# Attention and soft experts on one core: another order of the attention's steps and loads, and one cast split between ScalarE and GpSimd

## The chip, the cores and the metric

The kernel runs on one core of a Trainium2 chip. The metric is the time of one execution on the device in microseconds (us); lower is better. The engines go by their short names: PE is TensorE's matmul, PEld its weight load, DVE is VectorE, ACT is ScalarE, POOL is GpSimd, SP is SyncE, which issues the transfers (DMAs).

## The reference

Attention over q, k, v of shape (4, 8, 768, 64): 4 batches, 8 heads, 768 positions. Each query sees the first 8 keys and the 96 keys up to its own position; a bias proportional to the distance, with a slope of its own for each head, is added. Then a mixture of 8 experts with 4 slots each, in which every slot is a softmax-weighted sum over all 3072 tokens:

```python
scores = scale * (q @ k.T) + bias            # masked outside the window
a = exp(scores - max); a /= a.sum(-1) + 1e-9
x = (a @ v) as 3072 x 512                    # heads side by side
logits = x @ phi                             # 512 x 32 slots
slot_input = softmax(logits, axis=0).T @ x   # over all tokens
slot_out = relu(slot_input @ w1[e]) @ w2[e]  # w1: 512 x 1024, w2: 1024 x 512
out = softmax(logits, axis=1) @ slot_out
```

The weights are 32 MB in float32, the queries, keys and values some 20 MB as laid out, the output 6 MB.

## The kernel before

**Units.** The 32 heads are taken in 16 pairs (units u = 0 to 15, four to a batch; i = 0, 1 is the head of the pair). A unit's work is cut into named steps, each a few instructions of one engine:

- `load_qk`, `load_v` (lines 424, 427): transfers of queries with keys (832 KB) and of values (448 KB) into one of two buffers each; units 2 and 3 have buffers of their own.
- `scores(u, k)`, k = 0, 1, 2 (L571, PE): 8, 8 or 12 float32 matmuls into one of two PSUM banks `sc`, in turn. `biased(u, k)` (L580, DVE): adds the bias table and keeps the running maximum, from the bank to `tb`, and so frees the bank.
- `max_t` (L587, PE), `max_r` (L592, DVE): the maximum over all, from `biased(u, 2)`. `exponential(u, i)` (L596, ACT): in place in `tb`.
- `w_hi(u, i)` (L599, ACT): the weights as float16, high part, into `ph`, for all three parts of 432 columns at once. `w_lo(u, i, part)` (L606): what the rounding left over, on POOL, or as `w_lo_dve` on DVE, for one part.
- `v_hi` (L539, POOL), `v_hi_act` (L542, ACT) or `v_hi_dve` (DVE), and `v_lo` (L549, DVE): the same split of the values.
- `values(u, i)` (L623, PE): 39 float16 matmuls, high by high, high by low, low by high. There is one buffer `ph` for each i, so `w_hi(u+1, i)` waits for `values(u, i)`; v_hi and v_lo have two, so unit u waits for values of u-2.
- `ev_sums`, `ev_recs` (or `ev_sum`, `ev_rec` for one head) and `ev_mul` (L639, L645, L651, DVE): divide by the sums, into `xn`. `tr(u, k)` (L663, PE): transposes; `tr_copy(u, k)` (L668, ACT) or `tr_copy_dve` (L672, DVE): out of PSUM, 480 columns for k = 0 and 288 for k = 1. `logits` (L693, PE) and, once a batch, the running softmax over tokens: `logits_all`, `strip_max`, `strip_exp`, `by_token`, `dispatch`.
- `warm` (L560, PE): matmuls on constants, at the start.

**What sets the order.** `ORDER` (line 55) is one list of all these steps. The program walks it and issues each step's instructions on its engine, so each engine's queue holds its steps in the list's order, and an instruction that waits holds all behind it on that engine. SP's queue holds the transfers in the list's order too: `load_qk`, `load_v`, and the pieces of the experts' weights: `piece(k)` (1 MB into one of ten free tiles), `extra(i)` (the unused ends of tiles still in use) and `free(i)` (a tile, or a part of one, of which the attention has made its last use). All run through `load_w` (line 413).

**After the list.** `last_dispatch` finishes the last batch, then comes the experts' part: `hidden_part` (L104: 128 matmuls of 512 columns), `project` (L159), the combination with the token weights (L205), copies out (L218) and the output's transfers (L221). In it, tiles whose w1 part is used up take the last eight w2 pieces, in two halves each: 17 transfers on `wp`, the second halves last, which only the last projection reads.

Of the kernel before, what the change touches and what calls it, by code (L numbers as in the profile page):

```python
# [28 lines left out]
QW = KB + WIN  # L29
# [278 lines left out]
def tile_attention_moe(ctx: ExitStack, tc: tile.TileContext, qk, v, phi, w1, w2, nn, out):  # L308
    nc = tc.nc
# [58 lines left out]
    phi_ = [t[:, 0:PH].bitcast(F16) for t in pht]  # L368
# [11 lines left out]
    held = []  # L380
    for name, i, *_ in ORDER:
        if name == "free":
# [70 lines left out]
    def blocks(w):  # L453
        return w[:, 0:6 * PB].rearrange("p (s c) -> p s c", c=PB)
# [19 lines left out]
    def late_constants():  # L474
        nc.gpsimd.tensor_tensor(out=i4, in0=ident[:, 0:32], in1=ident[:, 32:64], op=ALU.add)
        nc.gpsimd.tensor_tensor(out=i4, in0=i4, in1=ident[:, 64:96], op=ALU.add)
        nc.gpsimd.tensor_tensor(out=i4, in0=i4, in1=ident[:, 96:128], op=ALU.add)
        nc.gpsimd.tensor_copy(out=by_row.rearrange("p (s j) -> p s j", s=4), in_=ident.rearrange("p (s r) -> p s r", s=4)[:, :, 0:NS // 4])
        nc.gpsimd.memset(sl, 0.0)
        moe.constants()  # L480
# [18 lines left out]
    def tb(u):  # L499
        return tbuf[u % 3]  # L500
# [53 lines left out]
    def warm_x(u):  # L554
        for n in (256, 256, P):
            nc.tensor.matmul(out=xx[:, 0, 0:n], lhsT=idb[:, 0:P], rhs=idb[:, 0:n], start=True, stop=True)
# [31 lines left out]

    def max_r(u):
        m = ms.pop((u, "m"))[:, 0:P]  # L590
        nbs[u] = nb = wk.tile([P, 1], F32, name="nb", tag="nb", bufs=2)
        nc.vector.tensor_tensor_reduce(out=m, in0=m, in1=shift.to_broadcast([P, P]), scale=-T_SC, scalar=3.0e38, op0=ALU.add, op1=ALU.min, accum_out=nb)  # L592

    def exponential(u, i):
        t = tb(u)[:, i]
        nc.scalar.activation(out=t, in_=t, func=AF.Exp, bias=nbs[u], scale=T_SC)  # L596

    def w_hi(u, i):
        nc.scalar.copy(out=blocks(phi_[i])[:, :, 0:QW], in_=tb(u)[:, i].rearrange("p (s c) -> p s c", c=QW))  # L599

    def w_hi_dve(u, i):
        nc.vector.tensor_copy(out=blocks(phi_[i])[:, :, 0:QW], in_=tb(u)[:, i].rearrange("p (s c) -> p s c", c=QW))

    def w_lo(u, i, part, engine=None):
        c = slice(2 * part, 2 * part + 2)
        (engine or nc.gpsimd).tensor_tensor(out=blocks(plo_[i])[:, c, 0:QW], in0=tb(u)[:, i].rearrange("p (s c) -> p s c", c=QW)[:, c],  # L606
                                            in1=blocks(phi_[i])[:, c, 0:QW], op=ALU.subtract)

    def w_lo_dve(u, i, part):
        w_lo(u, i, part, nc.vector)  # L610

    def values(u, i):
        ph, pl = phi_[i], plo_[i]
        vh, vl = vhi[u % 2], vlo[u % 2]
        x = sums(u, i)
        ops = []
        for t in range(NJ):
            for j, c in ((t, PCOL[t]), (t - 1, PCOL[t - 1] + KB)):
                if j >= 0:
                    for w, vv, d in ((ph, vh, D + 1), (ph, vl, D), (pl, vh, D + 1)):  # L620
                        ops.append((t, c, w, vv, j, d))
        for z, (t, c, w, vv, j, d) in enumerate(ops):
            nc.tensor.matmul(out=x[:, (D + 1) * t:(D + 1) * t + d], lhsT=w[:, c:c + P], rhs=vv[:, j, i, 0:d],  # L623
                             start=(z == 0), stop=(z == len(ops) - 1), skip_group_check=True)
# [253 lines left out]

    def table_rest_act(u):
        table.rest(nc.scalar.copy)  # L880

    def table_pair_act(p):
        table.pair_act(p)

    def table_pair(p):
        table.pair(p)

    steps = dict(piece=piece_of, free=free, extra=extra, load_phis=load_phis, bcast=bcast, keys=keys, table_rest=table_rest, table_rest_act=table_rest_act, table_pair_act=table_pair_act, warm_x=warm_x, warm=warm,
                 table_even=table_even, table_odd=table_odd, table_pair=table_pair, load_qk=load_qk, load_v=load_v, v_hi=v_hi, v_hi_act=v_hi_act, v_hi_dve=v_hi_dve, v_lo=v_lo,
                 scores=scores, biased=biased, max_t=max_t, max_r=max_r, exponential=exponential, w_hi=w_hi, w_lo=w_lo, w_lo_dve=w_lo_dve, w_hi_dve=w_hi_dve,  # L890
                 values=values, ev_sum=ev_sum, ev_rec=ev_rec, ev_sums=ev_sums, ev_recs=ev_recs, ev_mul=ev_mul, tr=tr, tr_copy=tr_copy, tr_copy_dve=tr_copy_dve,
                 logits=logits, logits2=logits2, logits_half=logits_half, logits_all=logits_all, strip_max=strip_max, strip_exp=strip_exp,
                 strip_sum=strip_sum, by_token=by_token, by_token_copy=by_token_copy, lnat_copy=lnat_copy, dispatch=dispatch, dispatch_sum=dispatch_sum)
    late_constants()
    for name, u, *args in ORDER:
        steps[name](u, *args)
    left = LeftBanks()
    put_rest = last_dispatch(left, lambda: warm_x(last))
    att.close()


    tail = ExitStack()
# [327 lines left out]
```

## Time and profile before

| | |
|---|---|
| median of 3 runs | 185.04 us (184.34 to 185.16) |
| profiled execution | 184.54 us, span 182.5 us |
| PE busy (x2805) | 170.5 us, 93% |
| PEld busy | 125.8 us, 69% |
| DVE busy (x378) | 141.6 us, 78% |
| ACT busy (x164) | 125.8 us, 69% |
| POOL busy (x129) | 97.2 us, 53% |
| moved by DMA | 61.41 MB, mean 337 GB/s |

The span is from the first to the last instruction of the profiled execution. A busy share is the engine's time in instructions; matmuls are pipelined, so PE's is not a measure of how full the array is. The granted clock of PE is full (2.4 GHz) as long as PE works. In the timeline a row is one step or a run of equal instructions, with its start, its length and, in brackets, the idle time before it and what ended it.

### The profile page before, as it was taken

To read this page: it belongs to the slowest core of one execution; us is meant where nothing else is said; L and a number is where in the kernel's file an instruction comes from. 1 tells how busy PE (TensorE), PEld (TensorE's weight loads), DVE (VectorE), ACT (ScalarE), POOL (GpSimd) and SP (SyncE) were. 2 spreads that over 40 slices of the span, in tenths; PEclk is the share of its full clock that TensorE was granted. 3 is DMA by queue.
4 is the path that set the end of the run, shared out by engine and by line. 5 is a ranking of instruction groups with operands and counts; after the bars stand their busy time and mean duration, and the time that the engine had idled before them with its cause. 6 is when DMAs were issued, how large, how long until landed. Compare 5 with 4: busy or idle time off the path is not lost.

```text
span 182.5 us, 6745 instructions
## 1 busy us (share of the span) xinstructions
PE 170.5 (93%) x2805; PEld 125.8 (69%) x2805; DVE 141.6 (78%) x378; ACT 125.8 (69%) x164; POOL 97.2 (53%) x129
## 2 busy tenths in 40 slices
PE   8999899999999999999999998999899999999820
PEld 2567689797878877979888986875533256677710
DVE  5999999999998989899999999987867303346430
ACT  3499989999989999988999999953302120345320
POOL 6926689859799498797998996750010000000000
PEclk9999999999999999999999999999999999999975
DMA  6999999958998956789887399999999999989892
GB/s 186 420 399 390 413 400 392 392 192 307 381 391 338 383 156 247 250 310 379 288 344 276 89 310 376 407 370 416 416 387 409 408 404 404 380 303 405 347 334 65
DMA packets 15306, 61.41 MB, mean 337 GB/s; under 512 B 1698, under 2 KB 2850, under 8 KB 13474
## 3 DMA queue, kind: packets, MB, share of 16 engines
q1 hardware_dynamic: 15264, 60.89, 87.8%
q8 instruction: 24, 0.39, 0.9%
q14 instruction: 16, 0.13, 0.2%
q10 hardware_dynamic: 2, 0.00, 0.0%
HBM read 54.59 MB, written 6.29 MB: 334 GB/s over the span
## 4 chain that ended last, share of the span: by engine, by line


## 5 line engine op out<-in xcount | busy, mean ns | idle before, releaser
L606 POOL TENSOR_TENSOR ph<-tb,ph 128x432 f16<-128x432 f32 x83 | 85.9, 1066 | 18.9 <-ACT ph L599 15.8
L596 ACT ACTIVATE tb<-tb,nb 128x1296 f32<-128x1296 f32 x32 | 43.7, 1374 | 0.9 <-DVE nb L592 0.8
L623 PEld LDWEIGHTS <-ph 128*128 128x128 f16 x1248 | 40.7, 97 | 4.2 <-issue 2.8
L599 ACT CAST ph<-tb 128x1296 f16<-128x1296 f32 x32 | 40.6, 1271 | 2.8 <-PE x L623 0.9
L623 PE MATMUL x<-v,ph 128*128 128x65 f16 (+1 forms) x1209 | 42.0, 193 | 0.3 <-POOL ph L606 0.2
L571 PE MATMUL sc<-raw 64*128 64x216 f32 (+1 forms) x392 | 40.8, 340 | 0.0
L571 PEld LDWEIGHTS sc<-raw 64*128 64x128 f32 x392 | 32.3, 186 | 6.0 <-issue 3.5
L651 DVE CUSTOM_DVE_ANT_1 xn<-x,rc 120x448 f32<-120x448 f32 x31 | 18.3, 622 | 2.1 <-PE m L774 1.6
L580 DVE CUSTOM_DVE_ANT_1 tb<-sc,tt,mx 128x864 f32<-128x864 f32 x16 | 17.8, 1115 | 1.1 <-DVE mx L580 0.5
L549 DVE SCALAR_TENSOR_TENSOR v<-vt,v 128x896 f16<-128x896 f32 x14 | 16.2, 1159 | 0.0
L663 PE MATMUL m<-ident,xn 120*128 120x120 f32 x98 | 14.7, 276 | 0.2 <-DVE xmax L651 0.2
L663 PEld LDWEIGHTS m<-ident,xn 120*128 120x128 f32 x98 | 10.0, 141 | 2.7 <-issue 1.5
L104 PE MATMUL hp<-wp,sl 128*32 128x512 f32 x80 | 10.9, 594 | 0.3 <-ACT sl L99 0.3
L606 DVE TENSOR_TENSOR ph<-tb,ph 128x432 f16<-128x432 f32 x13 | 9.6, 765 | 0.0
L580 DVE CUSTOM_DVE_ANT_1 tb<-sc,xtt,mx 128x864 f32<-128x864 f32 x8 | 8.9, 1115 | 0.4 <-DVE mx L580 0.2
L580 DVE CUSTOM_DVE_ANT_1 tb<-sc,xta,mx 128x864 f32<-128x864 f32 x8 | 8.9, 1112 | 0.2
L542 ACT ACTIVATE v<-vt 128x896 f16<-128x896 f32 x9 | 8.6, 951 | 0.0
L205 PE MATMUL cp<-sos,ct 32*128 32x128 f32 (+1 forms) x120 | 8.4, 334 | 0.2 <-ACT ph L218 0.2
L159 PE MATMUL o<-wp,ht 128*32 128x128 f32 x256 | 8.4, 275 | 0.0
L580 DVE CUSTOM_DVE_ANT_1 tb<-sc,tt 128x864 f32<-128x864 f32 x8 | 8.4, 1050 | 0.0
L159 PEld LDWEIGHTS o<-wp,ht 128*32 128x32 f32 x256 | 6.6, 109 | 1.5 <-issue 1.0
L910 POOL MEMSET ht<- 128x536 f32 x1 | 0.5, 544 | 13.1 <-PE ld L848 13.1
(235 smaller groups left out, 283.5 us busy)
## 6 DMA issues: line engine op xcount, KB each, us to landing
raw<-in_qk_dram SPq DMA_DIRECT2D x14, 832.0 KB, 5.7
wp<-in_w_dram SPq DMA_DIRECT2D x10, 1024.0 KB, 8.0
wp<-in_w_dram SPq DMA_DIRECT2D x15, 512.0 KB, 9.0
vt<-in_v_dram SPq DMA_DIRECT2D x14, 448.0 KB, 5.5
tb<-in_w_dram SPq DMA_DIRECT2D x3, 1024.0 KB, 8.1
wp<-in_qk_dram SPq DMA_DIRECT2D x2, 832.0 KB, 9.5
raw<-in_w_dram SPq DMA_DIRECT2D x2, 832.0 KB, 4.5
ph<-in_w_dram SPq DMA_DIRECT2D x2, 768.0 KB, 9.9
```

The lines of the kernel that those rows point to most:

```text
L104: self.nc.tensor.matmul(out=hp[n][32 * s:32 * s + 32, :], lhsT=slv(a, c, s), rhs=w1(4 * a + s, c // 2)[:, (c % 2) * DF + 512 * n:(c % 2) * ...
L159: nc.tensor.matmul(out=o[32 * s:32 * s + 32, o0:o0 + w], lhsT=ht[:, k:k + 32], rhs=w2(4 * a + s, half)[:, at:at + w], start=(a == 0 and c ...
L542: nc.scalar.activation(out=vhi[u % 2][:, :, :, 0:D], in_=vraws(u), func=AF.Copy, scale=V_SC)
L549: nc.vector.scalar_tensor_tensor(out=vlo[k].rearrange("p j i d -> p (j i) d"), in0=vraws(u).rearrange("p j i d -> p (j i) d"), scalar=V_SC ...
L571: nc.tensor.matmul(out=z[:, i, at:at + n], lhsT=r_[r, KCOL[j]:KCOL[j] + KR], rhs=r_[r, KW + KB * j:KW + KB * j + n], start=True, stop=True)
L580: nc.vector.tensor_tensor_reduce(out=tb(u)[:, :, BW * k:BW * k + BW], in0=sc[(3 * u + k) % 2][:, :, 0:BW], in1=table.unit(u % NP, k), scal ...
L596: nc.scalar.activation(out=t, in_=t, func=AF.Exp, bias=nbs[u], scale=T_SC)
L599: nc.scalar.copy(out=blocks(phi_[i])[:, :, 0:QW], in_=tb(u)[:, i].rearrange("p (s c) -> p s c", c=QW))
L606: (engine or nc.gpsimd).tensor_tensor(out=blocks(plo_[i])[:, c, 0:QW], in0=tb(u)[:, i].rearrange("p (s c) -> p s c", c=QW)[:, c], in1=bloc ...
L623: nc.tensor.matmul(out=x[:, (D + 1) * t:(D + 1) * t + d], lhsT=w[:, c:c + P], rhs=vv[:, j, i, 0:d], start=(z == 0), stop=(z == len(ops) - ...
L651: nc.vector.tensor_tensor_reduce(out=xnb[(u // 2) % 3][:, :, c:c + D], in0=by_query(u, i)[:, :, 0:D], in1=rcs.pop((u, i)).unsqueeze(2).to_ ...
L663: nc.tensor.transpose(out=m[:, at:at + KB], in_=xnb[(u // 2) % 3][:, t, P * (p % 2):P * (p % 2) + P], identity=ident[0:KB, 0:KB])
```

## The change

The list gets another order, on all engines. Some steps change engine: `v_hi` of units 8 and 9 goes from ScalarE to GpSimd, that of unit 10 from GpSimd to ScalarE and that of unit 15 from GpSimd to VectorE; of the 32 `tr_copy`, VectorE has 7 in place of 8, one of them with 480 columns in place of three; 13 of the 96 `w_lo` stay on VectorE, but others. `w_hi(15, 0)` is split: part 0 on ScalarE, parts 1 and 2 on GpSimd. The order in which SP issues pieces and loads from unit 6 on was

piece 4, piece 1, qk 6, piece 6, qk 7, piece 3, v 6, qk 8, piece 0, v 7, qk 9, piece 2, v 8, qk 10, piece 7, v 9, qk 11, v 10, qk 12, piece 5, v 11, qk 13, piece 9, v 12, qk 14, piece 8, v 13, qk 15, v 14, v 15

and becomes

qk 6, piece 4, qk 7, piece 1, v 6, piece 6, qk 8, v 7, qk 9, v 8, qk 10, piece 3, v 9, piece 0, qk 11, v 10, qk 12, piece 2, v 11, piece 7, qk 13, piece 5, v 12, piece 9, qk 14, v 13, piece 8, qk 15, v 14, v 15.

The order of the 18 `free` was 0, 14, 11, 1, 9, 3, 16, 4, 10, 7, 17, 6, 2, 8, 13, 5, 12, 15 and becomes 0, 14, 11, 9, 1, 3, 16, 4, 7, 10, 17, 2, 8, 15, 5, 12, 6, 13; which piece lies in which tile follows from it. `warm`, the number of matmuls, and all that comes after the list stay.

The list is one line in the code; here it is broken, and cut to its beginning, the steps around units 2 and 3, those around unit 10, and the last pairs:

```diff
 ORDER = [
-    ('load_qk', 0), ('load_v', 0), ('load_qk', 1), ('load_v', 1), ('load_v', 3), ('load_qk', 2),
-    ('extra', 8), ('bcast', 0), ('load_qk', 3), ('keys', 0), ('load_v', 2), ('extra', 1),
+    ('load_qk', 0), ('bcast', 0), ('load_v', 0), ('load_qk', 1), ('load_v', 1), ('load_v', 3),
+    ('load_qk', 2), ('extra', 8), ('load_qk', 3), ('keys', 0), ('table_even', 0), ('load_v', 2),
+    ('extra', 1), ('warm', 0, 6),
...
-    ('w_lo', 0, 0, 0), ('w_hi', 0, 1), ('max_r', 1), ('w_lo_dve', 0, 0, 2), ('scores', 2, 2), ('exponential', 1, 0), ('biased', 2, 1),
-    ('w_lo', 0, 1, 0), ('values', 0, 0), ('w_lo_dve', 0, 1, 1), ('scores', 3, 0), ('w_hi', 1, 0), ('w_lo_dve', 0, 1, 2), ('v_lo', 1),
-    ('values', 0, 1), ('exponential', 1, 1), ('w_lo', 1, 0, 0), ('biased', 2, 2), ('load_v', 5), ('extra', 4), ('w_lo', 1, 0, 1),
-    ('w_hi', 1, 1), ('piece', 4), ('ev_sums', 0), ('ev_recs', 0), ('max_t', 2), ('biased', 3, 0), ('scores', 3, 1),
-    ('extra', 3), ('w_lo', 1, 0, 2), ('extra', 7), ('v_hi_act', 2), ('ev_mul', 0, 0), ('extra', 2), ('scores', 3, 2),
+    ('w_lo', 0, 0, 0), ('scores', 2, 2), ('biased', 2, 2), ('v_lo', 1), ('w_lo', 0, 1, 0), ('w_lo', 0, 1, 2), ('values', 0, 0),
+    ('w_hi', 1, 0), ('load_qk', 4), ('w_lo', 1, 0, 0), ('exponential', 1, 1), ('w_lo', 1, 0, 1), ('w_lo', 1, 0, 2), ('values', 0, 1),
+    ('ev_sums', 0), ('w_hi', 1, 1), ('w_lo', 1, 1, 1), ('ev_recs', 0), ('scores', 3, 0), ('ev_mul', 0, 0), ('biased', 3, 0),
+    ('max_t', 2), ('v_hi_act', 2), ('scores', 3, 1), ('load_v', 5), ('extra', 4), ('scores', 3, 2),
...
-    ('load_v', 11), ('logits_all', 7), ('w_hi', 10, 1), ('w_lo', 10, 1, 0), ('v_lo', 10), ('values', 9, 0), ('v_hi_act', 11),
-    ('max_t', 11), ('scores', 12, 2), ('strip_max', 7), ('strip_exp', 7), ('w_lo', 10, 1, 1), ('ev_sums', 9), ('ev_recs', 9),
-    ('ev_mul', 9, 1), ('scores', 12, 1), ('ev_mul', 9, 0), ('max_r', 11), ('by_token', 7), ('w_lo', 10, 1, 2), ('w_hi', 10, 0),
-    ('values', 10, 1), ('load_qk', 13), ('by_token_copy', 7), ('biased', 12, 1), ('w_lo', 10, 0, 0), ('scores', 13, 0), ('exponential', 11, 1),
-    ('w_hi', 11, 1), ('w_lo', 10, 0, 2), ('lnat_copy', 7), ('w_lo', 11, 1, 0), ('w_lo', 11, 1, 2), ('w_lo_dve', 10, 0, 1), ('piece', 9),
-    ('load_v', 12), ('w_lo', 11, 1, 1), ('biased', 12, 2), ('v_lo', 11), ('values', 10, 0), ('ev_sums', 10), ('load_qk', 14),
-    ('exponential', 11, 0), ('w_hi', 11, 0), ('w_lo', 11, 0, 0), ('max_t', 12), ('max_r', 12), ('dispatch', 7),
...
+    ('max_t', 11), ('w_hi', 10, 1), ('v_lo', 10), ('w_lo', 9, 0, 1), ('values', 9, 0), ('scores', 12, 2), ('w_lo', 10, 1, 1),
+    ('w_lo', 10, 1, 2), ('max_r', 11), ('w_hi', 10, 0), ('exponential', 11, 1), ('ev_sums', 9), ('scores', 12, 1), ('by_token', 7),
+    ('ev_recs', 9), ('ev_mul', 9, 0), ('ev_mul', 9, 1), ('tr', 9, 1), ('by_token_copy', 7), ('v_hi_act', 11), ('w_lo_dve', 10, 1, 0),
+    ('values', 10, 1), ('lnat_copy', 7), ('w_lo', 10, 0, 1), ('piece', 7), ('w_lo', 10, 0, 0), ('biased', 12, 1), ('load_qk', 13),
+    ('scores', 13, 0), ('w_lo', 10, 0, 2), ('values', 10, 0), ('w_hi', 11, 1), ('w_lo', 11, 1, 2), ('w_lo', 11, 1, 0), ('w_lo', 11, 1, 1),
...
-    ('biased', 15, 2), ('tr', 10, 1), ('tr_copy', 10, 1), ('max_t', 15), ('ev_sums', 13), ('ev_recs', 13), ('ev_mul', 13, 0),
-    ('logits', 11), ('max_r', 15), ('ev_mul', 13, 1), ('tr', 13, 1), ('strip_sum', 3), ('logits_all', 11), ('strip_max', 11),
-    ('w_hi', 14, 0), ('tr_copy_dve', 13, 1), ('exponential', 15, 1), ('w_lo', 14, 1, 1), ('w_lo', 14, 1, 2), ('values', 14, 1), ('free', 9),
-    ('tr', 12, 1), ('strip_exp', 11), ('w_lo_dve', 14, 0, 1), ('w_lo', 14, 0, 0), ('w_hi', 15, 1), ('w_lo', 15, 1, 0), ('tr_copy', 12, 1),
-    ('by_token', 11), ('lnat_copy', 11), ('w_lo', 15, 1, 2), ('w_lo_dve', 14, 0, 2), ('values', 14, 0), ('tr', 12, 0), ('v_lo', 15),
-    ('by_token_copy', 11), ('dispatch', 11), ('free', 3), ('ev_sums', 14), ('ev_recs', 14), ('tr_copy_dve', 12, 0), ('free', 16),
-    ('ev_mul', 14, 1), ('exponential', 15, 0), ('w_hi', 15, 0), ('ev_mul', 14, 0), ('w_lo_dve', 15, 0, 1), ('w_lo_dve', 15, 0, 0), ('w_lo_dve', 15, 0, 2),
-    ('tr', 13, 0), ('free', 4), ('w_lo', 15, 1, 1), ('values', 15, 1), ('ev_sum', 15, 1), ('ev_rec', 15, 1), ('ev_mul', 15, 1),
-    ('values', 15, 0),
+    ('biased', 15, 2), ('free', 9), ('values', 13, 1), ('w_hi', 14, 1), ('strip_sum', 3), ('w_lo_dve', 14, 1, 1), ('w_lo', 13, 0, 2),
+    ('w_lo', 14, 1, 2), ('w_lo', 14, 1, 0), ('tr', 11, 1), ('tr', 11, 0), ('free', 1), ('tr_copy', 11, 1), ('tr_copy', 11, 0),
+    ('values', 13, 0), ('ev_sums', 13), ('ev_recs', 13), ('w_hi', 14, 0), ('max_t', 15), ('w_lo', 14, 0, 1), ('max_r', 15),
+    ('exponential', 15, 1), ('free', 3), ('logits', 11), ('ev_mul', 13, 0), ('ev_mul', 13, 1), ('logits_all', 11), ('strip_max', 11),
+    ('w_lo_dve', 14, 0, 0), ('tr', 12, 1), ('tr_copy', 12, 1), ('values', 14, 1), ('v_hi_dve', 15), ('v_lo', 15), ('strip_exp', 11),
+    ('w_hi', 15, 1), ('w_lo_dve', 15, 1, 0), ('w_lo_dve', 15, 1, 2), ('free', 16), ('tr', 13, 1), ('tr_copy', 13, 1), ('w_lo', 14, 0, 2),
+    ('by_token', 11), ('lnat_copy', 11), ('by_token_copy', 11), ('free', 4), ('values', 14, 0), ('free', 7), ('exponential', 15, 0),
+    ('w_hi_part_pool', 15, 0, 2), ('free', 10), ('w_hi_part', 15, 0, 0), ('w_lo_dve', 15, 1, 1), ('tr', 12, 0), ('ev_sums', 14), ('ev_recs', 14),
+    ('dispatch', 11), ('ev_mul', 14, 0), ('ev_mul', 14, 1), ('strip_sum', 7), ('free', 17), ('tr_copy', 12, 0), ('values', 15, 1),
+    ('tr', 13, 0), ('w_hi_part_pool', 15, 0, 1), ('w_lo_dve', 15, 0, 1), ('tr_copy', 13, 0), ('w_lo', 15, 0, 0), ('ev_sum', 15, 1), ('ev_rec', 15, 1),
+    ('tr', 14, 1), ('w_lo', 15, 0, 2), ('free', 2), ('ev_mul', 15, 1), ('values', 15, 0),
...
 ]
...
+    def w_hi_part(u, i, part, copy=nc.scalar.copy):
+        c = slice(2 * part, 2 * part + 2)
+        copy(out=blocks(phi_[i])[:, c, 0:QW], in_=tb(u)[:, i].rearrange("p (s c) -> p s c", c=QW)[:, c])
+
+    def w_hi_part_dve(u, i, part):
+        w_hi_part(u, i, part, nc.vector.tensor_copy)
+
+    def w_hi_part_pool(u, i, part):
+        w_hi_part(u, i, part, nc.gpsimd.tensor_copy)
...
```

## Rows read from the trace of the kernel before

**Rows 1.** Windows: stretch, length; busy us of PE, PEld, DVE, ACT, POOL; clock; DMA; GB/s

```profile
4.00:124.00 120.00, 118.37 (x2026) 96.72 (x2026) 113.27 (x291) 108.80 (x119) 94.27 (x112) 1.00 0.88 331
...
132.30:173.50 41.20, 40.57 (x674) 23.09 (x674) 18.01 (x47) 10.44 (x27) 0.54 (x1) 1.00 0.98 383
...
80.00:85.00 5.00, 5.00 (x111) 4.15 (x111) 4.92 (x15) 4.41 (x5) 3.63 (x5) 1.00 0.87 311
```

**Rows 2.** Timeline of PE, steps that nothing holds: start, us, what

```profile
6.04 1.73 PE L571 MATMUL sc<-raw 64*128 64x216 f32 x16
7.71 0.59 PE L560 MATMUL x<-const-bfloat16-1.0 128*1 128x512 bf16 x2
...
11.14 1.81 PE L571 MATMUL sc<-raw 64*128 64x216 f32 x20
12.88 1.25 PE L560 MATMUL x<-const-bfloat16-1.0 128*1 128x512 bf16 x5
...
46.68 1.00 PE L571 MATMUL sc<-raw 64*128 64x216 f32 x8
47.61 1.36 PE L623 MATMUL x<-v,ph 128*128 128x65 f16 x39
48.81 0.51 PE L663 MATMUL m<-ident,xn 120*128 120x120 f32 x3
```

**Rows 3.** Timeline of PE, steps that something holds

```profile
21.54 0.32 PE L587 MATMUL m<-ident,mx 128*128 128x128 f32 x1 [0.57 <-DVE mx L580]
21.79 2.10 PE L571 MATMUL sc<-wp 64*128 64x216 f32 x20
23.91 1.33 PE L623 MATMUL x<-v,ph 128*128 128x65 f16 x39
...
86.72 1.55 PE L623 MATMUL x<-v,ph 128*128 128x65 f16 x39
88.20 1.00 PE L571 MATMUL sc<-raw 64*128 64x216 f32 x8
```

**Rows 4.** Timeline of DVE around 20 and 103 us

```profile
18.27 1.18 DVE L606 TENSOR_TENSOR ph<-tb,ph 128x432 f16<-128x432 f32 x2
...
20.37 1.11 DVE L580 CUSTOM_DVE_ANT_1 tb<-sc,xta,mx 128x864 f32<-128x864 f32 x1
...
102.91 1.89 DVE L549 SCALAR_TENSOR_TENSOR v<-vt,v 128x896 f16<-128x896 f32 x1
```

**Rows 5.** Groups by line: what, count, busy us, mean ns, idle before

```profile
L606 POOL TENSOR_TENSOR ph<-tb,ph 128x432 f16<-128x432 f32 x83 | 85.9, 1066 | 18.9 <-ACT ph L599 15.8 <-DVE v L549 2.0 <-PE sc L571 1.1
L599 ACT CAST ph<-tb 128x1296 f16<-128x1296 f32 x32 | 40.6, 1271 | 2.8 <-PE x L623 0.9 <-POOL ph L606 0.6
L651 DVE CUSTOM_DVE_ANT_1 xn<-x,rc 120x448 f32<-120x448 f32 x31 | 18.3, 622 | 2.1 <-PE m L774 1.6
L549 DVE SCALAR_TENSOR_TENSOR v<-vt,v 128x896 f16<-128x896 f32 x14 | 16.2, 1159 | 0.0
L542 ACT ACTIVATE v<-vt 128x896 f16<-128x896 f32 x9 | 8.6, 951 | 0.0
L539 POOL TENSOR_SCALAR v<-vt 128x896 f16<-128x896 f32 x5 | 4.8, 955 | 3.4 <-PE x L623 2.8 <-DMA vt<-in_v_dram 0.6
L668 ACT COPY xtt<-m 128x480 f32<-128x480 f32 (+1 forms) x7 | 3.5, 513 | 0.8 <-PE m L663 0.8
```

**Rows 6.** Timeline of ACT and DVE at the last pair

```profile
117.97 1.40 ACT L596 ACTIVATE tb<-tb,nb 128x1296 f32<-128x1296 f32 x1
...
120.87 1.64 DVE L606 TENSOR_TENSOR ph<-tb,ph 128x432 f16<-128x432 f32 x3
```

**Rows 7.** Line 413 after 133 us (issue ns, first and last start, landing), PE's timeline

```profile
L413 SPq DMA_DIRECT2D wp<-in_w_dram x17: 327/328/1166, 135.0 to 151.6; - x17
...
DMA to landing us min/median/max: 7.3/9.0/11.0
...
167.96 2.17 PE L159 MATMUL o<-wp,ht 128*32 128x128 f32 x72
```

More of the change, by code (lines that the diff above doesn't have):

```diff
@@ L889, in tile_attention_moe @@
                  table_even=table_even, table_odd=table_odd, table_pair=table_pair, load_qk=load_qk, load_v=load_v, v_hi=v_hi, v_hi_act=v_hi_act, v_hi_dve=v_hi_dve, v_lo=v_lo,
-                 scores=scores, biased=biased, max_t=max_t, max_r=max_r, exponential=exponential, w_hi=w_hi, w_lo=w_lo, w_lo_dve=w_lo_dve, w_hi_dve=w_hi_dve,
+                 scores=scores, biased=biased, max_t=max_t, max_r=max_r, exponential=exponential, w_hi=w_hi, w_lo=w_lo, w_lo_dve=w_lo_dve, w_hi_dve=w_hi_dve, w_hi_part=w_hi_part, w_hi_part_dve=w_hi_part_dve, w_hi_part_pool=w_hi_part_pool,
                  values=values, ev_sum=ev_sum, ev_rec=ev_rec, ev_sums=ev_sums, ev_recs=ev_recs, ev_mul=ev_mul, tr=tr, tr_copy=tr_copy, tr_copy_dve=tr_copy_dve,
```

2 lines of the change are left out of this document (1 added, 1 removed).

## Prediction

> **What bounds the kernel now.** First the page: its busy shares put TensorE far ahead, but a share over the whole span hides the stages, so next the table of windows [rows 1]. From 4 to 124 us, the attention, TensorE is busy 118.37 of 120 us, VectorE 113.27, ScalarE 108.80, GpSimd 94.27: four engines near full, and the reader is to see that TensorE alone has almost no idle time. From 132.3 to 173.5 us, the experts' part, TensorE is busy 40.57 of 41.20 and nothing else is above half; no step of the change lies there. Between them are 8.3 us of small dependent steps.
>
> A busy matmul row need not mean that TensorE sets the pace, so I read its timeline step by step [rows 2]. scores(7,0) starts at 46.68 and hands over to values(4,1) at 47.61, which hands over to the next transposes at 48.81: 0.93 and 1.20 us from start to start, no gap. So in the attention the end is set by TensorE's own work plus the places where it is held. The clearest of those [rows 3]: 0.57 us of idle at 21.54, where max_t(2) waits for biased(2,2); scores(3,1) and scores(3,2), which take 2.12 us (21.79 to 23.91) where the same pair of another head pair took 1.74 (11.14 to 12.88) [rows 2]; values(10,1), 1.48 us (86.72 to 88.20) instead of 1.20. Idle time in 4 to 124 us is 1.63 us in all, 120 less 118.37; with the 0.38 and 0.28 us by which those two are drawn out, some 2.3 us is about all that a better order can win by holding TensorE less.
>
> **The change part by part.** Nothing is computed that was not computed before. What moves between engines, over the whole list [rows 5]: ScalarE loses one v_hi (0.95), two thirds of w_hi(15,0) (0.85 of 1.27) and one tr_copy of 288 columns, and gains two of 480 columns (0.51 each; the shorter one at most that): about -1.1 us. VectorE gains v_hi(15) and one short copy and loses two long ones, which about offset; v_hi on VectorE isn't in the trace. The same 896 elements took 0.95 us on ScalarE, 0.96 on GpSimd and 1.16 in VectorE's own two-input form. I take 0.95, the value that two one-input rows share, with 0.5 (half of it) and 1.2 as ends, so VectorE's total changes by about +0.2. GpSimd gains two part copies. Its 83 subtractions stay 83 and VectorE's 13 stay 13, in other places. With 1.1 us fewer on an engine that does not set the pace, little follows by itself.
>
> *TensorE's own pace.* Every step has as many matmuls as before. A scores step followed by scores or a transpose is 0.1 us shorter than one followed by values: 1.67 us for the two from 6.04 to 7.71 against 2 x 0.93 [rows 2]. The new list has 29 such followers for its 48 scores steps, the old one 25: -0.4 us.
>
> *Start.* biased(2,2) now stands ahead of v_lo(1) and of one of the two subtractions that ran from 18.27, so max_t(2)'s 0.57 us go. What is late next is the bank of scores(3,2): it needs biased(3,0), which in the new list follows biased(2,2) behind v_lo(1), the sums and ev_mul(0,0). From 18.27: one subtraction 0.6, biased 1.1, v_lo 1.1, sums 0.4 (estimated below the 0.62 of ev_mul, as they are tiny), ev_mul 0.6, biased 1.1 [rows 4, 5]: 23.1 us, or 22.9 with the small overlap of neighbours. scores(3,2) then hands over at about 24.0, against 23.91 now [rows 3]. So +0.1 us, not -0.6.
>
> *Around 86 us.* One of the three subtractions of values(10,1) goes to VectorE, which takes 1.07 us off the GpSimd queue ahead of it: its 0.28 us of stretch goes [rows 3, 5]. values(10,0) gets one more on GpSimd instead, so the queue is level again after it. -0.3 us.
>
> *Last pairs.* GpSimd no longer holds v_hi(15), behind which its subtractions for values(14,1) stood, and one of those moves to VectorE, so values(14,1) is held less. But exponential(15,0) comes on ScalarE behind the same sum of copies, within 0.2 us, so little of it reaches the end: -0.1.
>
> *The split high part.* Now: exponential(15,0) runs from 117.97 to 119.37; w_hi(15,0) follows with 1.27 and VectorE's three subtractions end at 122.51 (120.87 + 1.64), 3.1 us after the exponential [rows 6]. New: GpSimd copies parts 2 and 1 while ScalarE copies part 0, then GpSimd subtracts parts 0 and 2 and VectorE part 1. That copy on GpSimd is not in the trace: at the rate of its one-input v_hi it takes 0.46 us for 432 elements (0.955 x 432/896), as its two-input subtraction 1.07 [rows 5]. I take 0.5, by the one-input row, and keep both ends: 2 x 0.5 + 2 x 1.07 = 3.1 us, the same as now; 4.3 at the upper end. A gain is excluded beyond 0.1 us, since the two subtractions alone take 2.1 us behind a first copy and values(15,0) stands behind values(15,1) on TensorE anyway. So 0.
>
> On VectorE beside GpSimd the trace shows one v_lo of 1.89 us at 102.91 against a mean of 1.16 [rows 4, 5]. The Trainium skill (SBUF — State Buffer, Who interferes with whom) says that a VectorE instruction with two SBUF inputs and a GpSimd one that reads SBUF block each other wholly. The long row fits that; by the rule the part-1 subtraction could come a whole GpSimd instruction late, which the GpSimd chain beside it hides.
>
> *Loads.* Two of the ten early weight pieces move behind load_qk(11), so queries and values stand ahead of them on SP's one queue. Between 80 and 85 us the transfer engines are busy 0.87 at 311 GB/s [rows 1]; one more megabyte there is 3.3 us at that rate, and load_qk(14) serves scores of some 8 us later, so it is hidden. At the queue's end the last seventeen weight loads are issued from 135.0 to 151.6 us and land at most 11.0 us later, by 162.6, while the block of matmuls that reads the last of them starts at 167.96 [rows 7]. Over 5 us of cover: counting the queue's end earns nothing here, and a delay costs only what exceeds those 5 us.
>
> Sum: -0.4 + 0.1 - 0.3 - 0.1 + 0 = -0.7 us. The profiled execution took 184.54 us (the span of 182.5 and 2.0 around it) and would take 183.8; the median shown, 185.04, is 0.5 above it, so I forecast 185.04 - 0.7 = **184.3 us**. A change of 0.5% (0.93 us) is about what can be told from none, and the forecast lies inside that.
>
> **The rivals.**
> 1. *Most holds go.* If the new order meets TensorE's needs everywhere, 1.5 to 2 us of the 2.3 go, with the shorter pairs some 2 us: 183.0. For it: ScalarE's 1.1 us less. Against: VectorE at 113.27 of 120 leaves few places to pull a step forward.
> 2. *Pairs of scores meet a full bank: slower.* There are two score banks. 20 scores steps now follow another directly, 14 before; each can be held as the pair at 21.79 was, by 0.38 us. If all six new pairs are held, that is 6 x 0.38 = 2.3 us against the sum's 0.7: 185.04 + 1.6 = 186.6 us. It decides from five held pairs on. For it: a biased step (1.11 us at 20.37 [rows 4]) is longer than a scores step (0.93). Against: between pairs stand 2 to 3 us of other TensorE work, in which VectorE catches up.
> 3. *GpSimd's last chain is late.* At 1.07 us for each copy it is 1.1 us longer: 184.3 + 1.1 = 185.4 us. For it: f16 output in strided blocks, as in the subtraction. Against: only one input.
> 4. *VectorE is the bound.* If matmul rows say nothing and weight loads tell how full TensorE is, they are busy 96.72 of 120 us and VectorE 113.27 [rows 1]; the end then follows VectorE's sum, +0.2: 185.2 us. Against: the even starts of rows 2. The Trainium skill (Perfetto Trace Analysis, Identifying the Most-Contended Engine) judges TensorE by LDWEIGHTS share rather than matmul share, and so would name VectorE; the starts speak against it here.
>
> **How the numbers follow.** Forecast 0.41 (its own range 183.7 to 185.2), rival 1 0.22, rival 2 0.15, rival 3 0.12, rival 4 0.10. Faster than 184.1: all of rival 1 and 0.15 of the forecast's 0.41, together 0.37. Slower than 186.0: rival 2 and 0.05 from rivals 3 and 4, 0.20. The rest is 0.43. The range, 182.9 to 186.4, leaves out the far halves of rivals 1 and 2.
>
> **What would show it.** TensorE's idle time from 4 to 124 us at 1.2 to 1.6 us. max_t(2) without a wait, and a hold at scores(3,2) instead. values(10,1) at 1.2 us. The part copies on GpSimd at about 0.5 us. The last weights landing still over 4 us ahead of their reader. The prediction is wrong if TensorE's first expert matmul moves by more than 1.5 us from where it is, or if the experts' stage itself changes length.

## The result, and the profile after

The changed kernel takes 187.41 us (median of 4, 187.35 to 187.47), the kernel before, beside it, 184.89 (184.34 to 185.16): a ratio of 1.014, interval 1.0116 to 1.0165. It is 2.5 us slower, where 0.7 us faster was forecast, and 187.41 lies above the range. The profiled execution took 187.42 us with a span of 185.5, so all shown below is of a typical execution.

The windows of after, for [rows 1]; the second starts where the experts' first matmul now starts (135.50 us, 132.32 before):

```profile
4.00:124.00 120.00, 115.25 (x1962) 94.20 (x1963) 115.66 (x282) 107.72 (x118) 97.23 (x113) 1.00 0.88 322
...
135.30:176.50 41.20, 40.38 (x673) 22.94 (x674) 18.09 (x47) 10.54 (x27) 0.55 (x1) 1.00 0.96 379
```

TensorE's idle time in the attention is 4.75 us of 120 (it was 1.63), VectorE is busy 2.4 us more, and the experts' stage, entered 3.2 us later, is as full as it was. So the loss lies ahead of it. The groups by line of after, for [rows 5] (lines after 599 have moved by 10: L606 is now L616, L623 L633, L651 L661, L663 L673):

```profile
L616 POOL TENSOR_TENSOR ph<-tb,ph 128x432 f16<-128x432 f32 x83 | 90.0, 1115 | 18.1 <-ACT ph L599 18.0
...
L549 DVE SCALAR_TENSOR_TENSOR v<-vt,v 128x896 f16<-128x896 f32 x14 | 18.6, 1327 | 0.0
...
L580 DVE CUSTOM_DVE_ANT_1 tb<-sc,tt,mx 128x864 f32<-128x864 f32 x16 | 17.8, 1114 | 1.1 <-DVE mx L580 0.7 <-POOL ph L616 0.2
L616 DVE TENSOR_TENSOR ph<-tb,ph 128x432 f16<-128x432 f32 x13 | 12.4, 970 | 0.0
```

The same 13 low parts on VectorE stood in the trace of before, which showed no row of them ahead, as

```profile
L606 DVE TENSOR_TENSOR ph<-tb,ph 128x432 f16<-128x432 f32 x13 | 9.6, 765 | 0.0
```

Same counts, same shapes, other durations: v_lo went from 1159 to 1327 ns, VectorE's low parts from 765 to 970, while the bias step (L580), which reads PSUM, keeps 1114. In these rows VectorE computes nothing more than before; something holds it, and the experiments below show what. What TensorE waited for (line, releaser, us in total, times, longest):

```profile
PE x L633 <- DVE ph L616: 1.4, 2, 0.9
PE sc L571 <- DVE mx L580: 1.4, 1, 1.4
...
PE x L633 <- POOL ph L616: 0.7, 3, 0.3
```

And the place of the two longest waits (0.86 and 1.35 of the 4.75 us), the timelines of DVE, POOL and PE around 20 us, for [rows 3, 4]:

```profile
16.89 1.06 DVE L616 TENSOR_TENSOR ph<-tb,ph 128x432 f16<-128x432 f32 x1
...
19.12 1.41 DVE L616 TENSOR_TENSOR ph<-tb,ph 128x432 f16<-128x432 f32 x1
20.45 1.10 DVE L580 CUSTOM_DVE_ANT_1 tb<-sc,xta,mx 128x864 f32<-128x864 f32 x1
...
21.49 1.53 DVE L549 SCALAR_TENSOR_TENSOR v<-vt,v 128x896 f16<-128x896 f32 x1
...
23.96 1.05 DVE L580 CUSTOM_DVE_ANT_1 tb<-sc,xtt 128x864 f32<-128x864 f32 x1
...
18.09 1.98 POOL L616 TENSOR_TENSOR ph<-tb,ph 128x432 f16<-128x432 f32 x2 [0.60 <-ACT ph L599]
21.06 5.72 POOL L616 TENSOR_TENSOR ph<-tb,ph 128x432 f16<-128x432 f32 x5 [0.99 <-ACT ph L599]
...
20.59 1.02 PE L633 MATMUL x<-v,ph 128*128 128x65 f16 x28 [0.86 <-DVE ph L616]
...
25.08 1.07 PE L571 MATMUL sc<-wp 64*128 64x216 f32 x12 [1.35 <-DVE mx L580]
```

Two of GpSimd's subtractions run from 18.09 to 20.07. VectorE's, which starts at 19.12, ends at 20.53, 0.46 us after them: it does nearly all of its 0.60 us once GpSimd is done. values(0,1) stops 0.86 us for it; the same again at 21.49 makes biased(3,0) end at 25.02, and scores(3,2) stands idle 1.35 us.

### The profile page after: what moved, and what is told of

Read it like the earlier page. It is cut to its first block, busy times and chain, and to the rows that moved or that the text cites. A ratio compares the mean times of both kernels' runs of the same rounds, so it can differ in the third digit from the quotient of the medians.

```text
span 185.5 us, 6754 instructions
## 1 busy us (share of the span) xinstructions
PE 170.4 (92%) x2805; PEld 126.0 (68%) x2805; DVE 146.4 (79%) x378; ACT 125.3 (68%) x164; POOL 102.2 (55%) x131
## 4 chain that ended last, share of the span: by engine, by line
## 5 line engine op out<-in xcount | busy, mean ns | idle before, releaser
L616 POOL TENSOR_TENSOR ph<-tb,ph 128x432 f16<-128x432 f32 x83 | 90.0, 1115 | 18.1 <-ACT ph L599 18.0
L633 PEld LDWEIGHTS <-ph 128*128 128x128 f16 x1248 | 41.2, 97 | 6.9 <-issue 2.9
L633 PE MATMUL x<-v,ph 128*128 128x65 f16 (+1 forms) x1209 | 42.7, 193 | 2.9 <-DVE ph L616 1.4
L599 ACT CAST ph<-tb 128x1296 f16<-128x1296 f32 x31 | 39.1, 1271 | 4.8 <-PE x L633 3.7
L571 PE MATMUL sc<-raw 64*128 64x216 f32 (+1 forms) x392 | 39.7, 338 | 0.2
L661 DVE CUSTOM_DVE_ANT_1 xn<-x,rc 120x448 f32<-120x448 f32 x31 | 18.4, 621 | 0.9 <-PE m L784 0.2
L580 DVE CUSTOM_DVE_ANT_1 tb<-sc,tt,mx 128x864 f32<-128x864 f32 x16 | 17.8, 1114 | 1.1 <-DVE mx L580 0.7
L549 DVE SCALAR_TENSOR_TENSOR v<-vt,v 128x896 f16<-128x896 f32 x14 | 18.6, 1327 | 0.0
L673 PE MATMUL m<-ident,xn 120*128 120x120 f32 x98 | 14.9, 275 | 0.4 <-DVE xtt L682 0.3
L616 DVE TENSOR_TENSOR ph<-tb,ph 128x432 f16<-128x432 f32 x13 | 12.4, 970 | 0.0
L673 PEld LDWEIGHTS m<-ident,xn 120*128 120x128 f32 x98 | 10.0, 141 | 3.2 <-issue 1.4
L580 DVE CUSTOM_DVE_ANT_1 tb<-sc,xtt,mx 128x864 f32<-128x864 f32 x8 | 8.9, 1112 | 0.4 <-DVE mx L580 0.2
L580 DVE CUSTOM_DVE_ANT_1 tb<-sc,xta,mx 128x864 f32<-128x864 f32 x8 | 8.9, 1110 | 0.3
L580 DVE CUSTOM_DVE_ANT_1 tb<-sc,tt 128x864 f32<-128x864 f32 x8 | 8.4, 1051 | 0.6 <-PE sc L571 0.5
L542 ACT ACTIVATE v<-vt 128x896 f16<-128x896 f32 x8 | 7.6, 950 | 0.0
L159 PE MATMUL x<-ph,ht 128*32 128x256 f32 x32 | 7.2, 380 | 0.0
```

The source lines that it names most:

```text
L159: nc.tensor.matmul(out=o[32 * s:32 * s + 32, o0:o0 + w], lhsT=ht[:, k:k + 32], rhs=w2(4 * a + s, half)[:, at:at + w], start=(a == 0 and c ...
L549: nc.vector.scalar_tensor_tensor(out=vlo[k].rearrange("p j i d -> p (j i) d"), in0=vraws(u).rearrange("p j i d -> p (j i) d"), scalar=V_SC ...
L571: nc.tensor.matmul(out=z[:, i, at:at + n], lhsT=r_[r, KCOL[j]:KCOL[j] + KR], rhs=r_[r, KW + KB * j:KW + KB * j + n], start=True, stop=True)
L580: nc.vector.tensor_tensor_reduce(out=tb(u)[:, :, BW * k:BW * k + BW], in0=sc[(3 * u + k) % 2][:, :, 0:BW], in1=table.unit(u % NP, k), scal ...
L661: nc.vector.tensor_tensor_reduce(out=xnb[(u // 2) % 3][:, :, c:c + D], in0=by_query(u, i)[:, :, 0:D], in1=rcs.pop((u, i)).unsqueeze(2).to_ ...
L673: nc.tensor.transpose(out=m[:, at:at + KB], in_=xnb[(u // 2) % 3][:, t, P * (p % 2):P * (p % 2) + P], identity=ident[0:KB, 0:KB])
```

## The experiments

The kernel before ran again beside each group of them, with medians of 184.6 to 184.9 us; each ratio is against those runs.

**Both orders without GpSimd's reads.** The two kernels with the same edit:

```diff
-    tensor_tensor(out=plo[:, c, 0:QW], in0=tb[:, c], in1=phi[:, c], op=subtract)   # gpsimd
+    tensor_tensor(out=plo[:, c, 0:8], in0=tb[:, c, 0:8], in1=phi[:, c, 0:8], op=subtract)
+    for _ in range(2):
+        memset(plo[:, c, 8:QW], 0.0)
```

> The kernel before, but each of GpSimd's 83 weight subtractions (L606) is a subtraction of 8 columns of each 216 and two memsets of the others: GpSimd waits for the same things and is busy about as long (estimate 0.15 + 2 x 0.45 us against 1.07), but reads almost nothing. The low part of the weights is left out for those columns. Theory C (GpSimd's subtractions hold VectorE's two-input subtractions): v_lo falls from 1159 ns to about 1080 and VectorE's w_lo from 765 to about 600, and the time is 183.5 to 185 us, since the order of before meets little of it. Rival D (the order, not contention, makes the difference): v_lo may fall too, the time is 184.9 within 0.5. If memsets hold VectorE as subtractions do, v_lo stays at 1159 or more and this pair of runs says nothing.

> The changed kernel with the same edit. Theory C: v_lo falls from 1327 to about 1080 ns, VectorE's w_lo from 970 to about 600, and most of the 2.5 us go: 184.5 to 185.5 us, at most 0.8 above the same edit in the kernel before. Rival D (the new order's places in the queues cost the time, whatever the durations): v_lo falls all the same, but the time stays 2 to 3 us above the other, 186.5 to 187.4 us.

Old order 185.63 us (ratio 1.0041, 1.0019 to 1.0063), new order **183.28 us** (0.9917, 0.9885 to 0.9948). Groups by line of the new order with fills (there L617 is the low part, L621 its memsets, L637 values):

```profile
L621 POOL MEMSET ph<- 128x416 f16 x166 | 74.4, 448 | 4.8
...
L617 POOL TENSOR_TENSOR ph<-tb,ph 128x16 f16<-128x16 f32 x83 | 20.7, 249 | 12.6 <-ACT ph L599 12.4
...
L549 DVE SCALAR_TENSOR_TENSOR v<-vt,v 128x896 f16<-128x896 f32 x14 | 15.2, 1086 | 0.0
L617 DVE TENSOR_TENSOR ph<-tb,ph 128x432 f16<-128x432 f32 x13 | 7.7, 604 | 0.5 <-ACT ph L599 0.4
```

Its window of the attention (columns as in [rows 1]):

```profile
4.00:124.00 120.00, 117.23 (x2045) 97.53 (x2044) 111.18 (x293) 108.68 (x122) 96.87 (x280) 1.00 0.89 337
```

TensorE is idle 2.77 us there, not 4.75; 0.76 of the 2.77 stand ahead of scores(0,2), because this execution started its first scores early, at 5.26 us. GpSimd is busy as long as before (249 + 2 x 448 = 1145 ns for each low part, even more than 1115), in the same places of the queues, behind the same waits. Only its reading is gone, and both of VectorE's groups fall to one value, 1086 and 604 ns (1088 and 603 in the old order). With holds the new order is 2.5 us slower than the old, without them 2.35 us faster. So the loss is the holds, not the new dependences: the rival that the order itself is slow has fallen. The fills have a price of their own (the old order got 0.77 us slower with them). Both times miss their ranges, the old order's above 183.5 to 185 us, the new one's below 184.5 to 185.5; the durations came as theory C had them. The price falls on both orders, but that it is equal is not shown: a low part on GpSimd became 70 ns longer in the old order (1066 to 248 + 2 x 444) and 30 in the new. So 2.35 is no exact worth of the order; that the new order itself gains 4.1 us with them (187.41 to 183.28), though GpSimd gets busier, does not depend on it. GpSimd was held as well: its low part took 1066 ns in the mean before and 1115 after, and 1.01 us alone in the next run. The fills take away both sides at once, so how much of the loss came by VectorE's holds and how much by GpSimd's stays open. VectorE's held time, in the two groups: 18.6 + 12.4 - 15.2 - 7.7 = 8.1 us after, 16.2 + 9.6 - 22.9 = 2.9 before.

**What holds what.** A list of pairs, one instruction on each engine, released together by a copy on ScalarE; the later one is kept back by a small copy ("lead") of 0.2 us on its engine:

```diff
+for p in (none, two, copy, fill):            # GpSimd: two inputs, one input, memset
+    for d in (none, two, copy, scaled, bank):  # VectorE: bank = one operand in PSUM
+        lead on VectorE; p on GpSimd; d on VectorE
+for p in (two, copy, fill): for d in (two, copy, bank): d on VectorE; lead and p on GpSimd
```

> Not the attention: a list of pairs of one GpSimd and one VectorE instruction of 128 x 432 that become ready together, GpSimd first in some, VectorE first in others (the output is left out). Theory C as a lock (who starts second waits until the first has ended): a two-input subtraction on VectorE (0.60 us alone) takes 1.2 to 1.5 us when GpSimd's started up to 0.3 us earlier, and ends about 0.6 us behind it; in the other order GpSimd's takes 1.3 to 1.5 instead of 1.01. Rival: both share a bandwidth, then both are stretched by similar factors and neither waits for the other's end. An addition with one operand in PSUM, and a memset on GpSimd, should meet no hold by the first runs (biased L580 kept 1114 ns in every kernel); of the copies with one input no run has shown anything yet.

Its timelines, VectorE's first:

```profile
4.48 0.60 DVE L322 TENSOR_TENSOR do_two<-a,hi 128x432 f16<-128x432 f32 x1
...
5.99 0.38 DVE L325 CAST do_copy<-a 128x432 f16<-128x432 f32 x1
...
11.85 1.41 DVE L322 TENSOR_TENSOR do_two<-a,hi 128x432 f16<-128x432 f32 x1
...
14.17 1.19 DVE L325 CAST do_copy<-a 128x432 f16<-128x432 f32 x1
...
18.37 0.60 DVE L331 TENSOR_TENSOR do_bank<-pb,a 128x432 f32<-128x432 f32 x1
...
29.57 0.60 DVE L322 TENSOR_TENSOR do_two<-a,hi 128x432 f16<-128x432 f32 x1
...
11.78 1.01 POOL L322 TENSOR_TENSOR po_two<-a,hi 128x432 f16<-128x432 f32 x1 [0.76 <-ACT a L342]
14.10 1.01 POOL L322 TENSOR_TENSOR po_two<-a,hi 128x432 f16<-128x432 f32 x1 [1.31 <-ACT a L342]
...
29.77 0.46 POOL L334 MEMSET po_fill<- 128x432 f16 x1
...
35.70 0.68 POOL L346 COPY lead<-a 128x64 f32<-128x64 f32 x1 [0.79 <-ACT a L342]
...
40.23 0.24 POOL L346 COPY lead<-a 128x64 f32<-128x64 f32 x1 [0.74 <-ACT a L342]
```

VectorE's subtraction takes 0.60 us alone (4.48). Started 0.07 us behind GpSimd's (11.78, ends 12.79), it ends at 13.26, 0.47 us behind that end. GpSimd's own 1.01 is not stretched at all. So it is a lock, not a shared rate: who comes second waits for the first to end. A one-input copy on VectorE is held just so (0.38 alone, 1.19 at 14.17), an operand in PSUM is not (18.37), and beside a memset on GpSimd nothing on VectorE is (29.57). In the other order GpSimd waits: its 0.24 us copy (40.23, beside the PSUM form) takes 0.68 when VectorE's subtraction came first (35.70). The Trainium skill (SBUF — State Buffer, Who interferes with whom) says this, down to the memset; here its rule holds with these numbers. The 1.3 to 1.5 us expected of GpSimd's subtraction in that order did not come (1.00), since the small copy ahead of it had done the waiting.

**Where in the order.** Half of the order from each kernel:

```diff
-ORDER = <changed order>
+ORDER = <order of before up to ('values', 1, 0)> + <the changed order's other steps>   # startB_restA
+ORDER = <changed order up to ('values', 1, 0)> + <the order of before's other steps>   # startA_restB
```

> The order of before up to the step values(1,0), about the first 26 us, and from there the changed order. Rival S (all is lost in the first 26 us, where the trace of after lags 2.2 us, and carried to the end): 184.9 us within 0.5. Theory C with contention spread over the whole order: part of it returns, 185.5 to 186.3 us. If the start is of no account: 187.4 us.

> The counterpart: the changed order up to values(1,0), then the order of before. Rival S: 187 us. Theory C spread over the order: 186 to 186.8 us. If a late start is made up later in the slack of the order of before: 184.9 to 185.5 us.

186.16 us (1.0076, 1.0050 to 1.0103) and 186.64 us (1.0096, 1.0060 to 1.0131): a new start alone costs 1.8 us, a new rest alone 1.3. Both times lie where theory C had them; rival S, with all the loss in the start, had 184.9 for the first and is out. With the new start TensorE waits 1.34 us for the bank of scores(3,2), as in the changed kernel; with the old one scores(3,2) hands over at 23.91, as in the kernel before, and it is max_t(2) that waits, 0.57 us. Next, GpSimd's reads taken out of the first two pairs alone, and out of all others alone:

```diff
-    n = 8                        # columns that GpSimd subtracts, as above
+    n = 8 if u < 2 else QW       # fill_first
+    n = 8 if u >= 2 else QW      # fill_later
```

> The changed kernel with GpSimd's subtractions of the first two pairs alone (11 of its 83, among the first 26 us) turned into an 8-column subtraction and two memsets; the low part of those weights is left out. Theory C: VectorE's w_lo(0,0,1), w_lo(0,1,1) and v_lo(1), held 0.46, 0.81 and 0.45 us there, run in 0.60, 0.60 and 1.08, scores(3,2) stops waiting (1.35 us), and 1.0 to 1.6 us come back: 185.6 to 186.3 us. If the first pairs' holds are made up later anyway: 186.8 to 187.4 us.

> The counterpart: GpSimd's subtractions of pairs 2 to 15 are turned into fills, those of the first two pairs stay. Theory C: the wait of scores(3,2) stays and the rest of the holds goes, so 1.3 us above the 183.28 of all fills: 184.3 to 185.0 us. If the gain of the fills came from something else than the holds (the last pairs alone, say), the two runs would not add up to it.

185.93 us (1.0076, 1.0050 to 1.0102) and 185.85 us (1.0056, 1.0035 to 1.0077). In the trace the first two pairs have 10 subtractions on GpSimd, not 11. The first run gives back 1.5 us, within the 1.0 to 1.6 expected; in its timeline of PE the hold of scores(3,2) is down from 1.35 to 0.27 us:

```profile
22.72 1.08 PE L571 MATMUL sc<-wp 64*128 64x216 f32 x12 [0.27 <-DVE mx L580]
23.73 1.35 PE L637 MATMUL x<-v,ph 128*128 128x65 f16 x39
```

The second is a miss: 1.6 us back, not 2.4 to 3.1. The two add up to 3.0, all fills gave 4.1; by the expectation's own sign this leaves room for a cause beside the holds. In its trace the late start makes GpSimd's chain of longer fills late as well (TensorE waits 1.6 us for it between 24 and 50 us, 0.7 with all fills), which would explain a part, but no run tests it; where the last microsecond comes from stays open.

**Moving work off the lock.** Seven of VectorE's 13 low parts given to GpSimd, and four of GpSimd's five scalings of v given to ScalarE, in the new order and in the old:

```diff
-('w_lo_dve', u, i, part)      # pairs 0 to 12
+('w_lo', u, i, part)          # gp_all
-('v_hi', u)                   # u = 1, 7, 8, 9 of the new order; 1, 7, 10, 15 of the old
+('v_hi_act', u)               # after_vact; before_vact
```

> The changed kernel with the 7 low parts that VectorE has in pairs 0 to 12 given to GpSimd; VectorE keeps v_lo and the 6 of the last two pairs. Theory C: VectorE loses 7 instructions of 0.98 to 1.41 us and some 4 us of holds, so if GpSimd has room (it was idle 22.8 of the 120 us from 4 to 124) 185.5 to 186.5 us. If GpSimd's room is used up, since 7 more of 1.01 us stand in front of TensorE's values: 187.4 us or more, with TensorE waiting for GpSimd's low parts where it waited for VectorE's.

> The changed kernel with four of GpSimd's five scalings of v (pairs 1, 7, 8 and 9, 0.94 us each) on ScalarE. Theory C, as a lock that GpSimd's and VectorE's SBUF work share (held by one or the other for all but some 4 us between 20 and 120 us in the trace of after): 3.8 us of locked time go, VectorE's and GpSimd's holds shrink, 185.5 to 186.7 us. Rival: ScalarE, busy 107.7 of the 120 us, takes 3.8 us more and its high parts come later: 187.4 us or more.

> The kernel before with four of its five scalings of v (pairs 1, 7, 10 and 15) on ScalarE. Theory C: little to gain, since TensorE was idle only 1.6 of the 120 us: 184.1 to 184.9 us. Rival ScalarE late: 185.3 us or more.

192.36 us (1.0421, 1.0389 to 1.0452), 187.34 (1.0130, 1.0107 to 1.0154) and 187.10 (1.0131, 1.0110 to 1.0153). The first is 5.0 us slower than the changed kernel; TensorE's waits in it:

```profile
PE x L633 <- POOL ph L616: 8.0, 9, 1.8
```

GpSimd had 22.8 us of idle time in the window, but not where TensorE needs the low parts: values(0,0) alone ended at 20.78 instead of 18.75 us. My 185.5 to 186.5 was read from a busy share, and wrong. Taking 3.8 us of GpSimd's work away with the scalings bought nothing in the new order, where 0.7 to 1.9 was expected: VectorE's two groups still took 30.9 us, after 31.0, with v_lo at 1.36 in the mean. In the old order it costs 2.3 us; the rival, ScalarE late, had 185.3 or more, and TensorE's wait of a max_t for a copy on ScalarE grew from 0.4 to 1.2 us. ScalarE's added work stands in both times, so they do not price the lock. What the trace of after_vact does show is that less work on GpSimd did not by itself mean less holding: which instructions meet counts, not their sum.

**The split.** Undone in the new order, and made alone in the old:

```diff
-w_hi_part_pool(15,0,2), w_hi_part(15,0,0), w_hi_part_pool(15,0,1), w_lo(15,0,0), w_lo(15,0,2)
+w_hi(15,0), w_lo_dve(15,0,0), w_lo_dve(15,0,2)      # split_undone; before_split is the reverse, and has w_lo(15,1,1) ahead of the copies
```

> The changed kernel with the last pair's high part (15,0) whole on ScalarE and its three low parts on VectorE, as before. My forecast for the split was 0. By the trace of after its last low part took 1.45 us on GpSimd behind VectorE's last subtraction: theory C expects 0.3 us back (range 0 to 0.6), so 187.1 us; if the split was a gain that the holds hid, 187.6 us.

> The order of before with the split alone: the high part (15,0) as two thirds on GpSimd and one on ScalarE, and its low parts 0 and 2 on GpSimd as in the changed kernel. My forecast for the split was 0 (184.7 us). Theory C: the order of before does not wait for ScalarE there (its VectorE began the low parts straight after ev_mul(14,0)), while GpSimd takes 1.01 us for a low part where VectorE takes 0.60, and the two lock each other: 0.2 to 0.9 us slower, 184.9 to 185.6 us.

187.69 us (1.0166, 1.0142 to 1.0191) without it in the new order, where the changed kernel, run beside it, took 187.14 and in the first result 187.41: the split is a gain of 0.3 to 0.5 there, little above the noise, and my expectation of a loss was wrong. Alone in the old order it costs 1.5 us: 186.36 (1.0090, 1.0070 to 1.0110). Its timelines there:

```profile
121.88 1.39 DVE L616 TENSOR_TENSOR ph<-tb,ph 128x432 f16<-128x432 f32 x1 [0.99 <-POOL ph L603]
...
122.86 1.00 PE L633 MATMUL x<-v,ph 128*128 128x65 f16 x21 [0.86 <-POOL ph L616]
```

VectorE's low part waits for GpSimd's copy, is then locked out by GpSimd's subtraction (1.39 for 0.60), and values(15,0) waits for GpSimd twice, 0.86 us and then 0.33.

**The changed kernel again**, unaltered:

> The changed kernel once more, unaltered, beside the others. If the start of the first scores (6.72 us in the trace of after, 6.04 before, 5.26 to 6.67 in the first four runs) is a chance of each execution and no effect of the order, it lies elsewhere in that range here, while VectorE's subtractions are held as long as before: v_lo 1.33 and w_lo 0.97 us in the mean; time 187.4 us.

187.14 us (1.0140, 1.0117 to 1.0163); v_lo 1330 ns, VectorE's low parts 970. The means repeat within 3 ns: the holds follow from the order and are no accident of one execution.

No version that computes everything beat the kernel before, so none is offered.

## Why the prediction was wrong, point by point

*TensorE sets the pace, with some 2.3 us of holds to win.* Right of the kernel before, but used one way only: an engine with no slack can lose as much as its neighbours can be late, and it lost 3.1 us (idle 1.63 to 4.75). The first expert matmul moved by 3.2 us, more than the 1.5 that the prediction named as its sign of being wrong.

*VectorE's total changes by about +0.2.* **This is the step that failed**, and with it the whole sum, which has no term for holds between VectorE and GpSimd. The page has VectorE at 146.4 us after and 141.6 before, +4.8; v_lo and the low parts alone grew from 25.8 to 31.0. I counted instructions and gave them the durations they had in the old order. VectorE's v_lo and low parts have no duration of their own: 1.08 and 0.60 us, plus what is left of GpSimd's instruction. [rows 4] held the evidence, one v_lo of 1.89 us against 1.16, and I named the rule that explains it, but applied it to the split alone and let "the GpSimd chain beside it" hide it. A new order moves 29 such instructions (16 v_lo, 13 low parts) against 83 of GpSimd's, and each meeting has to be looked at.

*Start, +0.1.* The wait moved from max_t(2) to scores(3,2), as said. The sum to the end of biased(3,0), 22.9 us, was made with [rows 4]'s unhindered 0.6 and 1.1; it came at 25.02. Of the 2.1 us, 0.68 is the later start of this execution's scores(0,0) (6.72 against 6.04); most of the rest are two holds, 1.41 - 0.60 = 0.81 and 1.53 - 1.08 = 0.45. Without holds, in fill_first, scores(3,2) handed over at 23.73, where 24.0 was forecast. In the second run of the changed kernel, whose first scores started at 5.94, it handed over at 25.44, 1.5 us behind the kernel before: that much is not the start's doing. The chain was right, its durations were not.

*TensorE's own pace -0.4, around 86 us -0.3, last pairs -0.1.* No run shows them one by one. Together, the sum of -0.7 is what I said the order is worth; without the holds the new order stands 2.35 us ahead, with the reserve on the fills' price above. values(10,1) took 1.31 us from start to the next step (89.97 to 91.28) instead of 1.48, so 0.17 of the 0.28 us came back there.

*The split, 0.* GpSimd's part copies, and v_hi(15) on VectorE, in the timelines of POOL and DVE:

```profile
122.66 1.04 POOL L603 CAST ph<-tb 128x432 f16<-128x432 f32 x2 [3.76 <-DVE ph L616]
123.65 2.42 POOL L616 TENSOR_TENSOR ph<-tb,ph 128x432 f16<-128x432 f32 x2
...
119.28 0.62 DVE L545 TENSOR_SCALAR v<-vt 128x896 f16<-128x896 f32 x1
```

The copies took 0.5 each, as forecast (the row shows two), v_hi 0.62 where I took 0.95 within 0.5 to 1.2. The chain was forecast at 3.1 us and took 3.4, since GpSimd's last subtraction was locked out by VectorE's. So 0 held of neither order: 0.3 to 0.5 us of gain in the new, 1.5 of loss in the old.

*Loads, 0.* Right: no wait of TensorE in the attention of after ends with a DMA. The weights of the queue's end and their reader, for [rows 7]; first line 413 after 136 us:

```profile
L413 SPq DMA_DIRECT2D wp<-in_w_dram x17: 327/328/917, 138.1 to 155.4; - x17
...
DMA to landing us min/median/max: 7.8/9.0/11.4
```

And in the timeline of PE:

```profile
171.15 2.17 PE L159 MATMUL o<-wp,ht 128*32 128x128 f32 x72
```

They land by 155.4 + 11.4 = 166.8, 4.3 us ahead of their reader, and the reader moved by 3.2 us, no more than the attention's end did.

*The rivals.* Rival 2 had 186.6, the nearest number, by a mechanism that was there only as a consequence of the holds. Three pairs of scores met a full bank: scores(3,2) stood idle 1.35 us, and the pairs at 50.88 and 102.15 took 2.09 and 2.03 us where one at 36.82 took 1.80. Each followed a held instruction of VectorE (1.53, 1.93 and 0.98 us), and without GpSimd's reads the last two pairs took 1.80. The rival needed five. Rival 3's long copies did not come (0.5 us), and rival 4 had the right engine for the wrong reason: VectorE's sum grew by holds, 4.8 us, not by 0.2 of work. Rival 1's 183.0 is close to what the order gives when GpSimd does not read (183.28). The rival that was missing is the rule of the Trainium skill that stood in the text (SBUF — State Buffer, Who interferes with whom), taken for the whole order.

## What to carry to other kernels

Before a new order is priced, find the instructions whose duration depends on what runs beside them: a group whose longest row is far above its shortest, on VectorE with its operands in SBUF, beside GpSimd. Such an instruction costs its own time plus what is left of the other's, so a planner with fixed durations will trade a visible wait for an invisible one; with the holds and without them the same new order stood 2.5 us behind the old and 2.35 ahead. If work is to move, read room on an engine at the place of need, not from its share. To give VectorE what reads PSUM, and to keep SBUF-only work where the two engines don't meet, follows from the pairs; no run here tried it on the whole kernel.

## What the runs showed that was not expected

A one-input copy on VectorE, too, waits for GpSimd (0.38 us becomes 1.19); I had thought of two-input forms only. And the start of the first scores differs between executions, whatever the order: the six matmuls ahead of them took 2.72 us in after, by its timeline of PE:

```profile
4.07 2.72 PE L560 MATMUL x<-const-bfloat16-1.0 128*1 128x512 bf16 x6
```

In the same kernel run again they took 1.94 us:

```profile
4.07 1.94 PE L560 MATMUL x<-const-bfloat16-1.0 128*1 128x512 bf16 x6
```

And in the new order with fills 1.46 us:

```profile
3.87 1.46 PE L560 MATMUL x<-const-bfloat16-1.0 128*1 128x512 bf16 x6
```

The granted clock reads 1.00 in all three. values(0,0) ended at 18.75 us for starts of scores(0,0) at 5.26, 5.94 and 6.04, and at 19.39 for 6.72: some of the spread is taken up, and up to 0.6 us of a profile's difference is this alone. So it is with the 3.2 us above: in the second run of the changed kernel the first expert matmul starts at 134.88, 2.6 us behind the kernel before, and not at 135.50.
